# Score products of 48 by 128 instead of 48 by 64 in five pairs of a fused attention and feed-forward kernel

## The chip, the cores and the metric

The kernel runs on one core of a Trainium2 chip. The metric is the device time of one execution in microseconds (us), the median of repeated runs. Beside it stands one profiled execution, from which every duration below is taken.

## What is computed

The reference runs a gated linear attention over 4 batches, 8 heads, 768 positions and head size 48, and then a feed-forward block over the 3,072 tokens that come out:

```python
f = 1.0 / (1.0 + np.exp(-f_logit))
for t in range(S):
    state = f[:, :, t, :, None] * state + np.einsum('bhd,bhe->bhde', k[:, :, t], v[:, :, t])
    y[:, :, t] = np.einsum('bhd,bhde->bhe', q[:, :, t], state)
...
h = x @ w_in          # 3072 x 384 times 384 x 2048
g = h * np.cos(h)
return (g @ w_out).astype(np.float32)   # times 2048 x 384
```

The kernel doesn't step through the positions. It takes the sequence in pieces of 128, multiplies q and k by their running gate products, forms all products of q and k inside a piece (the scores), masks them, and carries a 48 by 48 state from piece to piece.

## The kernel before

**Tiling.** Two pieces of 128 positions make a pair; there are 12 pairs, three for each batch. Inside a pair each tile has 128 partitions of two neighbouring positions (e = 0 or 1), the 8 heads are halved into u = 0 and 1, and within a half the four heads are two head pairs (a = 0 or 1) of two heads (r = 0 or 1). The two pieces of a pair are g = 0 and 1. After the gates, `qk` holds q and k of one pair, each head widened from 48 to 64 columns by zeros.

**Turning q and k.** The scores need q and k with the head size on the partitions. For pairs 5 to 11 (`TURN_QK`) a transposing DMA on SP's queue does this (line 427). For pairs 0 to 4 TensorE does it: steps `tq` and `tk` are four products with the identity each (line 438), one for each e (in the code x) and a, into a bank of PSUM, and step `qkt` on DVE or ACT copies the result to the SBUF tile `qkt`. A head with r = 0 then lies on partitions 0 to 47, one with r = 1 on 64 to 111.

**Scores.** Step `sc` (line 460) computes for one pair and one half u the scores of four heads and two pieces. There are two such steps for each pair, so 24 in all, 10 of them for the five pairs that TensorE turns. Each is a loop over a, g, r and x: x is the position's parity on the side of k. The weights are 64 columns of k (48 rows), the moving data the 128 columns of q, and the result goes to partitions 64x to 64x + 63 of the PSUM bank that belongs to r. So one step is 16 matmuls with 16 weight loads, and four different quarters of TensorE's array are named in turn: rows by r, columns by x. Step `am` on DVE multiplies the scores by the mask.

**The other products of a pair.** Step `ps` (line 490) forms the products of k and v for the state from weights of 64 rows by 64 columns. Steps `y` and `yi` (line 543) form the output from weights of 128 rows by 32 columns; `yi` also reads q from `qkt`. The gates' running sums (lines 378 and 384) and the feed-forward products use the whole array.

**Feed-forward.** Steps `h` (line 610) and `o` (line 632) are the two large products, with a cosine on ACT (line 615) and the multiplication on DVE (line 582) between them.

**What sets the order.** The string `ORDER` lists every step with its engine and its PSUM bank or banks; `emit` writes them out in that order, and each engine works its own list in order. TensorE's steps of the attention are put between `h` and `o` steps. In the first 21 us there is not enough work, and steps `zf` multiply zeros (line 268) to keep TensorE running.

**Names that are used below:** `sc0.0`, `sc0.1`, `sc1.1`, `sc1.0`, `sc2.1`, `sc2.0`, `sc4.0`, `sc4.1`, `sc3.0`, `sc3.1` are the ten score steps of the turned pairs, in TensorE's order. In that order `ps0.1` stands right ahead of `sc0.1`, `ps2.1` right behind `sc2.1`, and `ps4.1` right ahead of `sc3.0`.

Of the kernel before, what the change touches and what calls it, by code (L numbers as in the profile page):

```python
# [10 lines left out]
BF16 = mybir.dt.bfloat16  # L11
# [4 lines left out]
B, H, S, D = 4, 8, 768, 48  # L16
# [173 lines left out]
def describe(nc, cpool, ppool, q, k, v, f_logit, moe_w_in, moe_w_out, out):  # L190
# [3 lines left out]
    def tl(shape, dt, name):  # L194
        return cpool.tile(shape, dt, name=name)

    def copy(e, o, i):
        (nc.scalar.copy if e == "ACT" else eng(e).tensor_copy)(out=o, in_=i)  # L198
# [6 lines left out]
    ident = tl([128, 128], BF16, "ident")  # L205
# [5 lines left out]
    if nc is not None:  # L211
# [5 lines left out]
        for r in range(2):  # L217
            s = slice(64 * r, 64 * r + 64)
# [96 lines left out]
    def pair(n):  # L315
# [50 lines left out]
        if not cut:  # L366
            G.step(f"ad{n}", ("POOL",), lambda e: eng(e).tensor_add(  # L367
                out=sp.ap[:, 0, :, 0:D], in0=soft.ap[:, :, 0, :], in1=soft.ap[:, :, 1, :]), reads=[soft], writes=[sp])
# [23 lines left out]
        for nm, dst, dh, sc, w in (("eb", bt, bth, -1.0, HB + 4), ("ei", bi, bih, 1.0, HB)):  # L392
            if cut:
                for u in us:
                    G.step(f"{nm}{n}.{u}", ("ACT",), lambda e, u=u, dh=dh, sc=sc, w=w: nc.scalar.activation(
                        out=dh[u].ap, in_=pcs[u].ap[:, 0:w], func=AF.Exp, scale=sc),
                        reads=[pcs[u]], writes=[dh[u]], table="E")
            else:
                G.step(f"{nm}{n}", ("ACT",), lambda e, dst=dst, sc=sc, w=w: nc.scalar.activation(
                    out=dst.ap, in_=pcs[0].ap[:, 0:2 * (HB + 4)].rearrange("p (u n) -> p u n", u=2)[:, :, 0:w],  # L400
# [5 lines left out]
        for u in us:  # L406
            for j, (nm, src, dec) in enumerate((("qm", qh[u], bth[u]), ("km", kh[u], bih[u]))):
                G.step(f"{nm}{n}.{u}", ("POOL", "DVE"), lambda e, u=u, j=j, src=src, dec=dec: eng(e).tensor_mul(  # L408
                    out=qkp[u][j].ap[:, :, :, 0:D], in0=swap(src.ap),
# [11 lines left out]

        qkt = [Val(qktS), Val(qktS)]
        turned = n in TURN_QK
        qkv = lambda u: qkt[u].ap.rearrange("p (j e a g n) -> p j a g e n", j=2, a=2, g=2, e=2)
        for u in us:
            if turned:
                G.step(f"tq{n}.{u}", ("SP",), lambda e, u=u: nc.sync.dma_start_transpose(
                    out=qkt[u].ap.rearrange("p (b n) -> p b n", n=C),
                    in_=qk.ap[:, u].rearrange("p j e h d -> p (j e h d)")),
                    reads=[qkp[u][0], qkp[u][1]], writes=[qkt[u]])  # L430
                continue
            pt = Val(p1)

            def tr(e, u, j, pt):
                o = pt.ap.bitcast(BF16).rearrange("p (j e a n) -> p j e a n", j=2, e=2, a=2)
                for x in range(2):
                    for a in range(2):
                        nc.tensor.transpose(out=o[:, j, x, a, :], identity=ident,  # L438
                                            in_=qkp[u][j].ap[:, x, 2 * a:2 * a + 2, :].rearrange("p h d -> p (h d)"))
            for j in range(2):  # L440
                G.step(f"t{'qk'[j]}{n}.{u}", ("PE",), lambda e, u=u, j=j, pt=pt: tr(e, u, j, pt),
                       reads=[qkp[u][j]], writes=[pt], sums=True)
            G.step(f"qkt{n}.{u}", ("DVE", "ACT"), lambda e, u=u, pt=pt: copy(e, qkt[u].ap, pt.ap.bitcast(BF16)),
                   reads=[pt], writes=[qkt[u]])
# [5 lines left out]
        for u in us:  # L450
            sc = Val(p2)

            def scores(e, u=u, sc=sc):
                o = sc.ap.rearrange("p (r b n) -> p r b n", r=2, n=C)
                for a in range(2):
                    for g in range(2):
                        for r in range(2):
                            for x in range(2):
                                s, t = slice(64 * r, 64 * r + D), slice(64 * x, 64 * x + 64)
                                nc.tensor.matmul(o[t, r, 2 * a + g, :].rearrange("p (e n) -> p e n", e=2),  # L460
                                                 lhsT=qkv(u)[s, 1, a, g, x, :], rhs=qkv(u)[s, 0, a, g, :, :],
                                                 start=(a == 0 and g == 0), stop=(a == 1 and g == 1))
            G.step(f"sc{n}.{u}", ("PE",), scores, reads=[qkt[u]], writes=[sc])
            if n in CHUNKS:
                for g in range(2):
                    G.step(f"am{n}.{u}{g}", ("DVE",), lambda e, u=u, g=g, sc=sc: nc.vector.tensor_mul(
                        out=am[u].ap.rearrange("p r (a g) n -> p (r a) g n", g=2)[:, :, g, :],
                        in0=sc.ap.rearrange("p (y g m) -> p y g m", g=2, m=C)[:, :, g, :],
                        in1=pmask.rearrange("p a n -> p (a n)")[:, None, :].broadcast_to([128, 4, C])),
                        reads=[sc], writes=[amp[u][g]])  # L470
                continue
            G.step(f"am{n}.{u}", ("DVE",), lambda e, u=u, sc=sc: nc.vector.tensor_mul(  # L472
                out=am[u].ap.rearrange("p r b n -> p (r b) n"), in0=sc.ap.rearrange("p (y m) -> p y m", m=C),
                in1=pmask.rearrange("p a n -> p (a n)")[:, None, :].broadcast_to([128, 8, C])),
                reads=[sc], writes=[am[u]])
# [22 lines left out]
        for g in gs:  # L498
            view = lambda g=g: ps[g].ap[:, 0:HB].rearrange("p (a n) -> p a n", n=D)
            dense, new, sums = Val(sdS), Val(szS), ps[g].part(None)  # L500
            if carried is not None:
                G.step(f"st{n}.{g}", ("DVE",), lambda e, view=view, S0=carried: nc.vector.tensor_add(
                    out=view(), in0=view(), in1=S0.ap), reads=[sums, carried], writes=[sums])
# [68 lines left out]
        x = Val(xS)  # L572
# [73 lines left out]
    for n in range(PAIRS):  # L646
        pair(n)
# [108 lines left out]
```

## Time and profile before

| | us |
|---|---|
| median of 3 runs | 181.26 (181.18 to 181.77) |
| the profiled execution's own time | 180.39 |
| its span, first to last instruction | 178.1 |
| so outside the span | 2.3 |
| granted TensorE clock | 1.00 of full speed in all 40 slices |

In the profile, PE is the matmul side of TensorE and PEld its weight loads, which overlap the matmuls. Matmuls are pipelined, so the time of one (some 0.22 us for 128 moving columns) is a latency; how fast they follow one another is read from the timeline, where a row merges a run of like instructions: start, time from the first start to the last end, line, shape and count. "issue" names idle time of an engine that waited for nothing that the profile shows. DMA queue 1 carries the kernel's own transfers; the packets of the kind "instruction" are listed apart.

### The profile page before, as it was taken

The page shows a single profiled execution, that of the slowest core. Times are in us where ns is not written, and L with a number is a line of the kernel's source. Part 1 is how long each engine was busy: PE and PEld are TensorE (multiplying, and loading weights), DVE is VectorE, ACT ScalarE, POOL GpSimd, SP SyncE. Part 2 cuts the span into 40 slices and gives each one's busy share as a digit, 9 for nine tenths or more (in the row PEclk, how much of TensorE's full clock was granted, in tenths as well). Part 3 has the DMA queues.
Part 4 walks back from the last instruction along what each step waited for, and adds up shares of the span by engine and source line. Part 5 has one row for each costly group of instructions (what it writes and reads, how often), then busy time and mean ns, then how long its engine had stood idle before and what let it go on. Part 6 is the DMA issues. An engine that isn't in the chain of part 4 may idle for free.

```text
span 178.1 us, 5999 instructions
## 1 busy us (share of the span) xinstructions
PE 169.9 (95%) x2546; PEld 124.9 (70%) x2550; DVE 135.5 (76%) x196; ACT 137.7 (77%) x205; POOL 100.4 (56%) x128
## 2 busy tenths in 40 slices
PE   7999999999999989999999999899999999999991
PEld 2555598766877678866688766787867778687770
DVE  5588829988799988899799789889998746547211
ACT  5789998899999999999999897798962646364221
POOL 4044979975797969985979979899401000000000
PEclk9999999999999999999999999999999999999999
DMA  5999999999999969999999979883730030010044
GB/s 139 260 270 303 376 349 347 315 296 263 261 255 264 261 139 219 284 196 256 253 245 306 171 184 275 148 203 59 147 77 4 0 123 13 4 44 0 0 172 140
DMA packets 72282, 33.94 MB, mean 191 GB/s; under 512 B 65344, under 2 KB 70720, under 8 KB 72256
## 3 DMA queue, kind: packets, MB, share of 16 engines
q1 hardware_dynamic: 72256, 33.56, 76.9%
q8 instruction: 20, 0.33, 0.8%
q14 instruction: 6, 0.05, 0.1%
HBM read 25.17 MB, written 4.72 MB: 168 GB/s over the span
## 4 chain that ended last, share of the span: by engine, by line
PE 83%; ACT 5%; DVE 5%; DMA 3%; issue 2%; ACTq 0%; DVEq 0%
PE ps L610 34%; PE ps L632 33%; PE ps L543 5%; PE ps L460 3%; DVE am L472 3%; PE ps L438 2%; PE ps L490 2%; PE ps L268 2%; DMA f<-in_f_logit_dram 1%; PE ps L378 1%; DMA out_dram<-ot 1%; ACT sp L337 1%; ACT f L333 1%; ACT vt L198 1%; DVE g L582 1%
## 5 line engine op out<-in xcount | busy, mean ns | idle before, releaser
L582 DVE TENSOR_TENSOR g<-ps,co 128x1024 bf16<-128x1024 f32 x48 | 60.2, 1310 | 18.7 <-ACT co L615 18.5
L632 PE MATMUL ps<-w_out_bf,g 128*128 128x384 bf16 (+1 forms) x400 | 69.2, 320 | 0.0
L610 PE MATMUL ps<-x,w_in_bf 128*128 128x256 bf16 (+1 forms) x624 | 66.6, 264 | 0.5 <-DVE g L582 0.4
L615 ACT ACTIVATE co<-ps,halfpi 128x1024 bf16<-128x1024 f32 x48 | 51.7, 1113 | 18.4 <-PE ps L610 16.3
L610 PEld LDWEIGHTS <-w_in_bf 128*128 128x128 bf16 x624 | 56.5, 98 | 8.3 <-issue 0.5
L632 PEld LDWEIGHTS <-g 128*128 128x128 bf16 x400 | 37.0, 98 | 20.0
L472 DVE TENSOR_TENSOR am<-ps,pmask 128x1024 bf16<-128x1024 f32 x22 | 26.0, 1216 | 1.5 <-PE ps L460 1.4
L408 POOL TENSOR_TENSOR qk<-q,b 128x384 bf16<-128x384 f32 x18 | 17.8, 1007 | 3.2 <-DVE q L342 2.3
L408 POOL TENSOR_TENSOR qk<-k,bi 128x384 bf16<-128x384 f32 x16 | 16.3, 1029 | 5.3 <-issue 2.0
L198 POOL COPY vt<-vb 64x384 bf16<-64x384 bf16 x31 | 15.8, 520 | 2.0 <-PE ps L543 0.6
L268 PE MATMUL ps<-zero 128*128 128x512 bf16 x40 | 12.7, 430 | 1.5 <-DVE zero L204 1.2
L198 ACT COPY ot<-ps 128x384 f32<-128x384 f32 (+1 forms) x13 | 5.8, 451 | 8.8 <-PE ps L632 7.1
L517 POOL TENSOR_TENSOR sz<-sd,half 128x384 bf16<-128x384 bf16 x10 | 8.2, 828 | 7.6 <-DVE sd L507 7.2
L198 POOL CAST vb<-v 128x768 bf16<-128x768 f32 x9 | 7.4, 825 | 8.9 <-DMA v<-in_v_dram 8.8
L333 ACT ACTIVATE f<-f 128x768 f32<-128x768 f32 (+1 forms) x14 | 10.3, 748 | 2.7 <-DMA f<-in_f_logit_dram 2.6
L198 DVE CAST x<-ps 128x384 bf16<-128x384 f32 x16 | 8.5, 552 | 4.8 <-PE ps L543 4.7
L367 POOL TENSOR_TENSOR sp<-ls 128x384 bf16<-128x384 f32 x10 | 10.0, 1000 | 2.3 <-ACT ls L337 2.1
L198 DVE COPY ot<-ps 128x384 f32<-128x384 f32 (+1 forms) x13 | 6.7, 521 | 4.6 <-PE ps L632 4.5
L345 POOL TENSOR_TENSOR q<-f,q 128x384 f32<-128x384 f32 x9 | 9.4, 1039 | 0.6 <-ACT f L348 0.2
L460 PE MATMUL ps<-qkt 48*64 48x128 bf16 x384 | 9.0, 220 | 0.3 <-DVE qkt L198 0.3
L198 ACT COPY vt<-vb 64x384 bf16<-64x384 bf16 x17 | 8.5, 508 | 0.3
L507 DVE TENSOR_TENSOR sd<-ps,b 128x192 bf16<-128x192 f32 x20 | 7.1, 354 | 2.1 <-PE ps L490 1.3
(66 smaller groups left out, 189.4 us busy)
## 6 DMA issues: line engine op xcount, KB each, us to landing
v<-in_v_dram SPq DMA_DIRECT2D x12, 384.0 KB, 5.9
out_dram<-ot SPq DMA_DIRECT2D x22, 192.0 KB, 3.0
f<-in_f_logit_dram SPq DMA_DIRECT2D x10, 384.0 KB, 5.8
q<-in_q_dram SPq DMA_DIRECT2D x10, 384.0 KB, 5.6
k<-in_k_dram SPq DMA_DIRECT2D x10, 384.0 KB, 6.3
g<-in_moe_w_in_dram SPq DMA_DIRECT2D x4, 768.0 KB, 8.4
g<-in_moe_w_out_dram SPq DMA_DIRECT2D x4, 768.0 KB, 9.3
f<-in_f_logit_dram SPq DMA_DIRECT2D x4, 192.0 KB, 3.7
```

Of the source, the lines that this page charges most:

```text
L198: (nc.scalar.copy if e == "ACT" else eng(e).tensor_copy)(out=o, in_=i)
L268: G.step(f"zf{i}", ("PE",), lambda e, dump=dump: nc.tensor.matmul(dump.ap, lhsT=zero[:, 0:128], rhs=zero, start=True, stop=True), writes=[ ...
L333: nc.scalar.activation(out=flat(t.ap), in_=flat(t.ap), func=AF.Exp, scale=-1.0)
L345: eng(e).tensor_mul(out=w.ap[:, :, 0, :], in0=t.ap[:, :, 1, :], in1=w.ap[:, :, 0, :])
L367: G.step(f"ad{n}", ("POOL",), lambda e: eng(e).tensor_add(out=sp.ap[:, 0, :, 0:D], in0=soft.ap[:, :, 0, :], in1=soft.ap[:, :, 1, :]), read ...
L408: G.step(f"{nm}{n}.{u}", ("POOL", "DVE"), lambda e, u=u, j=j, src=src, dec=dec: eng(e).tensor_mul(out=qkp[u][j].ap[:, :, :, 0:D], in0=swap ...
L460: nc.tensor.matmul(o[t, r, 2 * a + g, :].rearrange("p (e n) -> p e n", e=2), lhsT=qkv(u)[s, 1, a, g, x, :], rhs=qkv(u)[s, 0, a, g, :, :], ...
L472: G.step(f"am{n}.{u}", ("DVE",), lambda e, u=u, sc=sc: nc.vector.tensor_mul(out=am[u].ap.rearrange("p r b n -> p (r b) n"), in0=sc.ap.rear ...
L582: nc.vector.tensor_mul(out=o.rearrange("p b (n e) -> p b e n", e=2), in0=ph.ap.rearrange("p (b e n) -> p b e n", e=2, n=64), in1=co.ap.rea ...
L610: nc.tensor.matmul(ph.ap[:, i * T:(i + 1) * T].rearrange("p (g t) -> p g t", t=C), lhsT=w_in_bf[:, kk, f0:f0 + 128], rhs=xa[:, :, kk, :], ...
L615: G.step(f"co{m}.{j}", ("ACT",), lambda e, ph=ph, co=co: nc.scalar.activation(out=co.ap, in_=ph.ap, func=AF.Sin, bias=halfpi), reads=[ph], ...
L632: nc.tensor.matmul(po.ap[:, 0:c1 - c0], lhsT=gap[:, j, i * C:(i + 1) * C], rhs=w_out_bf[:, j, c0:c1], start=(po.first and j == 4 * s), sto ...
```

## The change

In the five pairs that TensorE turns, `qkt` is laid out with the two parities of one head pair and piece side by side (j, a, g, e, n in place of j, e, a, g, n). The turning product now writes its 128 columns as two pieces of 64. With that, the 128 columns of k for one head and piece are contiguous, and the score step loads them as one set of weights: eight products of 48 by 128 in place of sixteen of 48 by 64, each writing all 128 partitions. For pairs 5 to 11 the layout and the sixteen products stay. `ORDER` isn't touched.

```diff
         qkt = [Val(qktS), Val(qktS)]
         turned = n in TURN_QK
-        qkv = lambda u: qkt[u].ap.rearrange("p (j e a g n) -> p j a g e n", j=2, a=2, g=2, e=2)
+        lay = "p (j e a g n) -> p j a g e n" if turned else "p (j a g e n) -> p j a g e n"
+        qkv = lambda u: qkt[u].ap.rearrange(lay, j=2, a=2, g=2, e=2)
...
             def tr(e, u, j, pt):
-                o = pt.ap.bitcast(BF16).rearrange("p (j e a n) -> p j e a n", j=2, e=2, a=2)
+                o = pt.ap.bitcast(BF16).rearrange("p (j a g e n) -> p j a g e n", j=2, a=2, g=2, e=2)
                 for x in range(2):
                     for a in range(2):
-                        nc.tensor.transpose(out=o[:, j, x, a, :], identity=ident,
+                        nc.tensor.transpose(out=o[:, j, a, :, x, :], identity=ident,
                                             in_=qkp[u][j].ap[:, x, 2 * a:2 * a + 2, :].rearrange("p h d -> p (h d)"))
...
                         for r in range(2):
-                            for x in range(2):
-                                s, t = slice(64 * r, 64 * r + D), slice(64 * x, 64 * x + 64)
-                                nc.tensor.matmul(o[t, r, 2 * a + g, :].rearrange("p (e n) -> p e n", e=2),
-                                                 lhsT=qkv(u)[s, 1, a, g, x, :], rhs=qkv(u)[s, 0, a, g, :, :],
+                            s = slice(64 * r, 64 * r + D)
+                            for t, w in [(slice(64 * x, 64 * x + 64), qkv(u)[s, 1, a, g, x, :]) for x in range(2)] if turned else [
+                                    (slice(0, 128), qkv(u)[s, 1, a, g, :, :].rearrange("p e n -> p (e n)"))]:
+                                nc.tensor.matmul(o[t, r, 2 * a + g, :].rearrange("p (e n) -> p e n", e=2), lhsT=w,
+                                                 rhs=qkv(u)[s, 0, a, g, :, :],
                                                  start=(a == 0 and g == 0), stop=(a == 1 and g == 1))
```

No engine's steps change places, but TensorE's list becomes shorter: 16 rows less for each of the ten steps, so 4,942 rows in place of 5,102. (In the changed kernel all lines behind the diff stand two further down: 460 becomes 462, 490 becomes 492, 543 becomes 545, 610 becomes 612.)

First place, TensorE where `sc2.1` ends and `ps2.1` begins. Before:

```order
L460 LDWEIGHTS qkt_0_130
L460 MATMUL ps_1_166<-qkt_0_130 64x128
L490 LDWEIGHTS qk_0_121
L490 MATMUL ps_2_167<-vb_0_124,qk_0_121 64x48
L490 LDWEIGHTS qk_0_121
```

Now, at the same place:

```order
L462 LDWEIGHTS qkt_0_130
L462 MATMUL ps_1_166<-qkt_0_130 128x128
L492 LDWEIGHTS qk_0_121
L492 MATMUL ps_2_167<-vb_0_124,qk_0_121 64x48
L492 LDWEIGHTS qk_0_121
```

The neighbours are the same; the score product beside the 64 by 64 product now spans all columns of the array.

Second place, TensorE's list counted from its start, rows 1,978 to 1,982, which lie behind the ten steps. Before, inside step `y3`:

```order
L543 MATMUL ps_3_168<-am_2_137,vt_0_127 32x128
L543 LDWEIGHTS vt_0_127
L543 MATMUL ps_3_168<-am_2_137,vt_0_127 32x128
L543 LDWEIGHTS vt_0_127
L543 MATMUL ps_3_168<-am_2_137,vt_0_127 32x128
```

Now, in the same rows, feed-forward products:

```order
L612 MATMUL ps_3_168<-x_1_147,w_in_bf_163 128x256
L612 LDWEIGHTS w_in_bf_163
L612 MATMUL ps_2_167<-x_0_146,w_in_bf_163 128x256
L612 LDWEIGHTS w_in_bf_163
L612 MATMUL ps_2_167<-x_0_146,w_in_bf_163 128x256
```

Behind the ten steps every instruction of TensorE stands 160 rows earlier than before.

## The prediction

> **What bounds the kernel now.** I read the page first: busy shares, then the chain that ended last.
>
> ```profile
> span 178.1 us, 5999 instructions
> ...
> PE 169.9 (95%) x2546; PEld 124.9 (70%) x2550; DVE 135.5 (76%) x196; ACT 137.7 (77%) x205; POOL 100.4 (56%) x128
> ...
> PE 83%; ACT 5%; DVE 5%; DMA 3%; issue 2%; ACTq 0%; DVEq 0%
> ```
>
> TensorE is busy for 95% of the span and holds 83% of the chain. Time taken from TensorE's list should come off the end, time added should go on it. "issue" is 2% of the chain, time in which nothing visible was waited for. Next the waits of TensorE alone (sum, times, longest):
>
> ```profile
> PE ps L543 <- issue: 1.3, 2, 0.8
> PE ps L268 <- DVE zero L204: 1.2, 1, 1.2
> PE ps L610 <- DVE g L582: 0.4, 1, 0.4
> PE ps L268 <- issue: 0.3, 2, 0.2
> PE ps L460 <- DVE qkt L198: 0.3, 1, 0.3
> ```
>
> The second row lies at the start and the last three before 28 us. What TensorE loses in its dense part is the first row: two stalls inside `y` and `yi` (L543), with no producer named.
>
> **The score steps themselves.** The timeline of TensorE (start, time, line, shape, count) shows how fast matmuls follow one another:
>
> ```profile
> 10.86 0.42 PE L460 MATMUL ps<-qkt 48*64 48x128 bf16 x16
> ...
> 16.97 0.62 PE L438 MATMUL ps<-ident,qk 128*128 128x128 bf16 x8
> ...
> 38.12 0.42 PE L460 MATMUL ps<-qkt 48*64 48x128 bf16 x16
> 38.37 0.41 PE L490 MATMUL ps<-vb,qk 64*64 64x48 bf16 x16
> ...
> 40.12 0.42 PE L460 MATMUL ps<-qkt 48*64 48x128 bf16 x16
> 40.47 0.34 PE L632 MATMUL ps<-w_out_bf,g 128*128 128x384 bf16 x1
> ...
> 59.32 0.44 PE L490 MATMUL ps<-vb,qk 64*64 64x48 bf16 x32
> 59.60 0.74 PE L460 MATMUL ps<-qkt 48*64 48x128 bf16 x32
> ```
>
> And the groups by line, with the mean of one matmul and one load:
>
> ```profile
> L460 PE MATMUL ps<-qkt 48*64 48x128 bf16 x384 | 9.0, 220 | 0.3 <-DVE qkt L198 0.3
> L438 PE MATMUL ps<-ident,qk 128*128 128x128 bf16 x80 | 7.2, 219 | 0.2 <-DVE qk L408 0.2
> ...
> L460 PEld LDWEIGHTS <-qkt 48*64 48x64 bf16 x384 | 6.2, 106 | 3.0 <-issue 1.6 <-DVE qkt L198 1.2
> L438 PEld LDWEIGHTS <-qk 128*128 128x128 bf16 x80 | 5.6, 98 | 2.7 <-DVE qk L408 0.8 <-POOL qk L408 0.3 <-issue 0.2
> ```
>
> Eight whole-array matmuls of 128 columns take 0.62; less one latency of 0.22, seven spacings are 0.40, so 0.057 each. Sixteen score matmuls take 0.42, so fifteen spacings are 0.20, or 0.013 each: four quarters of the array run together, four rounds of some 0.055. The new step has eight matmuls whose weights fill half the rows and all columns, r = 0 and r = 1 in turn into different banks. Run two at a time, that is again four rounds of 0.055. **Removed:** 80 loads and 80 matmuls; **gained in the array:** nothing. The bounds of this term: the two halves together, 0; the halves one after the other, 8 x 0.057 = 0.46 in place of 0.23 (4 x 0.057), so +0.23 for a step. I take 0, since r = 0 and r = 1 are among the four that run together now.
>
> A load of 128 columns has 98 ns against 106 for 64, and loads run beside matmuls; first loads may save up to 0.01 a step, bounds 0 to -0.1 over ten, I take 0. [...]
>
> **Writing the turned tile in two pieces** (80 matmuls): no row shows a split write. The nearest is L460, which reads its moving data in two pieces and has 220 ns against 219. Bounds: 0 to 80 x 1 ns = 0.1; I take 0. The copy `qkt` and `am` read and write as many elements as before.
>
> **Changed neighbours.** From L460 to L490 at 38.12 the next start comes 0.25 later; from L460 to the whole-array L632 at 40.12 it is 0.35. So a change in how the array is divided costs 0.10, and L460 and L490 now share a division. After the change they don't, at three places: 11.83, 38.37 and 59.60. The first lies among the zero products (L268), which are filler and hide it; if they didn't, 0.1 more. Cost +0.2, bounds 0 to 0.3.
>
> **The two stalls move with the list.** The timeline around them, and a piece of the chain for the pace of L543:
>
> ```profile
> 63.14 0.23 PE L543 MATMUL ps<-am,vt 128*32 128x128 bf16 x4
> 63.84 0.57 PE L543 MATMUL ps<-am,vt 128*32 128x128 bf16 x28 [0.48 <-issue]
> ...
> 110.85 0.29 PE L543 MATMUL ps<-qkt,sz 128*32 128x128 bf16 x8
> 111.95 0.41 PE L543 MATMUL ps<-qkt,sz 128*32 128x128 bf16 x16 [0.81 <-issue]
> ...
> 143.06 1.68 PE ps L543 x112
> ```
>
> At 1.68 / 112 = 0.015 each, the matmul at 63.84 was due at 63.14 + 4 x 0.015 = 63.20: lost 0.64. The one at 111.95 was due at 110.97: lost 0.98. Together **1.62 us**. What they wait for is in the DMA views: the page's row of the queue that carries instructions, then the same row in the windows 61.10 to 61.25 and 109.25 to 109.35:
>
> ```profile
> q8 instruction: 20, 0.33, 0.8%
> ...
> q8 instruction: 1, 0.02, 47.0%
> ...
> q8 instruction: 1, 0.02, 77.1%
> ```
>
> TensorE's 2,546 + 2,550 instructions over 20 packets are 255 a packet, so I take a packet for 256 instructions of TensorE's list. Each stall ends 2.6 to 2.7 after such a packet started. The windows say whether both stand at the same place in a packet (time, then busy and count of PE and PEld; a window also counts what is in flight at its start, which at 63.84 and 111.95 is nothing):
>
> ```profile
> 63.84:111.95 48.11, 47.30 (x767) 35.83 (x767) 41.91 (x56) 44.55 (x65) 40.98 (x50) 1.00 1.05 229
> ...
> 59.51:63.84 4.33, 3.85 (x154) 2.88 (x143) 4.19 (x8) 4.29 (x11) 3.95 (x6) 1.00 1.11 254
> 107.92:111.95 4.03, 3.22 (x136) 2.35 (x137) 3.65 (x6) 2.92 (x7) 3.97 (x6) 1.00 1.22 275
> 83.76:88.57 4.81, 4.81 (x126) 3.06 (x127) 4.00 (x5) 4.76 (x12) 4.67 (x7) 1.00 1.19 261
> 130.24:135.39 5.15, 5.15 (x133) 3.51 (x136) 4.61 (x8) 2.15 (x6) 0.83 (x1) 1.00 0.26 51
> ...
> 110.24:116.17 5.93, 5.12 (x144) 4.30 (x133) 5.08 (x10) 3.85 (x7) 5.27 (x7) 1.00 0.91 186
> 86.82:92.08 5.26, 5.26 (x129) 4.06 (x128) 4.28 (x9) 5.15 (x10) 5.05 (x7) 1.00 1.01 236
> ```
>
> From stall to stall there are 767 + 767 = 1,534 instructions, and six packets are 1,536. So both are the first instruction of a packet. Counting 128 loads back, the packet ahead of each began at 59.51 and 107.92 (second and third row): 4.33 and 4.03 from one packet's first instruction to the next one's, while the work between took only 3.7 and 3.05. My reading: when TensorE enters a packet, the next is ordered, and it is there 4.0 to 4.3 later; a packet full of tiny matmuls is used up sooner. The next shortest, 4.81 and 5.15 (rows four and five), ran without a stall.
>
> Now the list is 160 shorter from 60 us on, and the packets' edges fall 160 instructions further on in the old order. Counting the old trace that way, the edge ahead of 63.84 falls to 62.47, and the next to 70.25, among L610 products: nearly 8 us. The edges around the second stall fall to 110.24 and 116.17 (row six): 5.93 less the lost 0.98 is 4.95. Of the others behind 30 us the shortest is 5.26 (row seven). All are over 4.33, the tightest by 0.6, so both stalls go: **-1.62**. Does the gain last? Behind 64 us the largest waits are:
>
> ```profile
> DVE g L582 <- ACT co L615: 15.5, 14, 3.3
> ACT co L615 <- PE ps L610: 15.1, 17, 3.5
> ```
>
> DVE waits for ACT, and ACT for TensorE, so both come earlier with TensorE. Next to be late would be `g` before the `o` steps; bounds: all of 1.62 lasts, or 1.0.
>
> **Sum** against the profiled execution: 180.39 + 0 + 0.2 - 1.6 = 179.0. The median stands 0.87 above that execution; with the same -1.4 it becomes **179.9**.
>
> **The rivals.**
> - *The stalls stay or come back elsewhere.* The packet's lead is seen at only two stalls. If it needs 5 to 6 us at times, 110.24 or 86.82 stalls by up to 1, and the gain is spent: 181.3, from 180.8 to 181.6. For it: TensorE's loads have more small "issue" waits that I don't explain. If one stall goes alone: 181.26 + 0.2 - 0.64 or - 0.98, about 180.6.
> - *The halves take turns.* Each of the ten steps costs 0.23 more; the six from 38 us on lie on TensorE's dense path, so +1.4 to +2.3. The sum is then 181.3 to 182.2 with -1.4 for the rest, and 182.8 with all ten steps and only 1.0 gained from the stalls (-0.8 + 2.3). It ends slower once the steps cost 0.54 more than the rest gains: 1.9 together, or 0.19 of the 0.23 each. For it: no row shows half the rows with all columns. Against it: the four quarters at 0.013. [...]
> - *Fewer starts are cheaper.* If a start and not the array set the pace of 0.013, eight would spread over 0.10 in place of 0.20: 0.1 a step, 1.0 over ten, 178.9. Against it: L490 at 59.32 has 32 matmuls of 0.19 in 0.44, so 0.008 between starts. [...]
>
> **How the numbers follow.** Both stalls gone: 0.52, 179.4 to 180.4. One gone: 0.16, about 180.6. Stay or come back: 0.16. Turns: 0.14, a fifth of it under 181.8. Fewer starts: 0.02. A measurement tells 0.3%, 0.54 us, from no change: faster means under 180.72. Faster: 0.52 + 0.11 of the second case + 0.02 = 0.65; same: 0.05 + 0.14 + 0.03 = 0.22; slower: the rest, 0.13, nearly all of it turns. The range, 179.2 to 181.9, leaves out most of the turns, the case of fewer starts, and a margin of the first.
>
> **What would show it.** Right: no "issue" row of 0.4 or more on L545 in TensorE's waits; 19 instruction packets in place of 20; a step of eight still 0.40 to 0.42; the start after `sc2.1` 0.35 later. Wrong: a step of eight over 0.5 (turns), or an "issue" wait on another line (the packet's lead is longer than 4.3).

## The result, and the profile after

The changed kernel takes 178.71 us (median of 4 runs, 178.65 to 179.66) against 181.49 (181.18 to 181.77) before: ratio 0.986, 95% interval 0.982 to 0.990. The ratios here and below leave out runs that are more than 1.5% above the fastest of their kernel, while medians and ranges have all runs. It was forecast faster by 1.4 us; it is faster by 2.8, and 178.71 lies below the range.

The page of the changed kernel, the lines that answer to those of before:

```profile
span 177.4 us, 5843 instructions
...
PE 170.8 (96%) x2470; PEld 124.8 (70%) x2470; DVE 136.0 (77%) x196; ACT 137.7 (78%) x205; POOL 100.1 (56%) x128
...
q8 instruction: 19, 0.31, 0.8%
```

80 matmuls and 80 loads are gone (four matmuls have no record in the profile of before, so it counts 2,546 where it counts 2,550 loads), TensorE's busy time isn't smaller (170.8 us against 169.9), and the queue of instructions has 19 packets in place of 20. The waits of TensorE (sum, times, longest):

```profile
PE ps L268 <- DVE zero L204: 1.2, 1, 1.2
PE ps L634 <- ACT w_out_bf L198: 0.8, 1, 0.8
PE ps L612 <- POOL w_in_bf L198: 0.4, 1, 0.4
PE ps L378 <- ACT sp L337: 0.3, 2, 0.2
```

No "issue" row is left (rows of under 0.15 us aren't listed). Where the two stalls were, TensorE's timeline (start, time, line, shape, count) now runs through:

```profile
63.77 0.63 PE L545 MATMUL ps<-am,vt 128*32 128x128 bf16 x32
64.23 0.68 PE L545 MATMUL ps<-qkt,sz 128*32 128x128 bf16 x36
64.73 0.62 PE L545 MATMUL ps<-am,vt 128*32 128x128 bf16 x32
...
111.00 0.52 PE L545 MATMUL ps<-qkt,sz 128*32 128x128 bf16 x24
111.34 0.62 PE L545 MATMUL ps<-am,vt 128*32 128x128 bf16 x32
111.79 0.51 PE L545 MATMUL ps<-qkt,sz 128*32 128x128 bf16 x24
112.13 0.62 PE L545 MATMUL ps<-am,vt 128*32 128x128 bf16 x32
```

This profiled execution has a wait of its own, the second row of the waits above: `o` products wait 0.8 us near 38.7 us for the cast of `w_out`, and ACT's cast waited 2.0 us for a transfer. It is the slowest of the four runs (179.66; the others have 178.65 to 178.76). So the two profiled spans, 178.1 and 177.4, show only 0.7 us of the 2.8: the profile of before is from a run 1.1 us below its kernel's median (180.39 against 181.49), and that of after from one 0.95 above.

### The profile page after: what moved, and what is told of

Read it like the earlier page. It is cut to its first block, busy times and chain, and to the rows that moved or that the text cites. A ratio compares the mean times of both kernels' runs of the same rounds, so it can differ in the third digit from the quotient of the medians.

```text
span 177.4 us, 5843 instructions
## 1 busy us (share of the span) xinstructions
PE 170.8 (96%) x2470; PEld 124.8 (70%) x2470; DVE 136.0 (77%) x196; ACT 137.7 (78%) x205; POOL 100.1 (56%) x128
## 4 chain that ended last, share of the span: by engine, by line
PE 75%; DMA 11%; ACT 3%; DVE 3%; SPq 2%; POOL 2%; issue 1%; DVEq 0%; POOLq 0%
PE ps L634 33%; PE ps L612 28%; DMA g<-in_moe_w_in_dram 5%; DMA v<-in_v_dram 5%; PE ps L545 4%; PE ps L462 3%; SPq L286 2%; PE ps L492 2%; PE ps L268 2%; POOL w_in_bf L198 2%; DMA f<-in_f_logit_dram 2%; PE ps L439 1%; DVE am L474 1%; PE ps L378 1%; DVE qk L408 1%
## 5 line engine op out<-in xcount | busy, mean ns | idle before, releaser
L198 POOL COPY vt<-vb 64x384 bf16<-64x384 bf16 x31 | 15.3, 503 | 1.4
L268 PE MATMUL ps<-zero 128*128 128x512 bf16 x44 | 13.9, 426 | 1.2 <-DVE zero L204 1.2
L355 POOL TENSOR_TENSOR k<-k,f 128x384 f32<-128x384 f32 (+1 forms) x7 | 6.8, 973 | 4.1 <-DMA k<-in_k_dram 2.0
L462 PE MATMUL ps<-qkt 48*64 48x128 bf16 (+1 forms) x304 | 8.9, 219 | 0.1
```

The lines of the kernel that those rows point to most:

```text
L268: G.step(f"zf{i}", ("PE",), lambda e, dump=dump: nc.tensor.matmul(dump.ap, lhsT=zero[:, 0:128], rhs=zero, start=True, stop=True), writes=[ ...
```

## The experiments

Two theories. **P**: the time lies in where TensorE's list is cut into packets of 256 instructions (an estimate: 1,534 instructions from stall to stall, over six packets); the change matters because it makes the list shorter. **S**: the eight wider products are cheaper themselves.

### e1: the kernel before, once more

> The unchanged kernel once more, for a second profile. Both theories expect 181.5 us. Theory P (the time lies where TensorE's list is cut into packets of 256 instructions): the same two issue waits at L543 near 63.8 and 112 us, at the same instructions, and 20 packets; what its usual run has above the first profile (181.5 against 180.4) should show as a longer or a third wait. Theory S (the eight wider products are cheaper themselves) says nothing of these waits.

Measured: 181.64 (10 runs, 180.5 to 183.2), ratio to before 1.004 (0.9995 to 1.009). Waits and timeline of TensorE in this second profile:

```profile
PE ps L543 <- issue: 1.8, 2, 1.3
...
63.36 0.23 PE L543 MATMUL ps<-am,vt 128*32 128x128 bf16 x4
64.92 0.57 PE L543 MATMUL ps<-am,vt 128*32 128x128 bf16 x28 [1.33 <-issue]
```

Same two places: 4 matmuls of this block, then the stall, then 28, as in the first profile. But the first stall is 1.33 in place of 0.48, the second 0.47 in place of 0.81. The places are fixed, the lengths are not. The two stalls together are 0.5 longer than in the first profile, most of the 0.77 that this run is longer (181.16 against 180.39).

### e2: sixteen products, cuts of the changed kernel

`EXTRA = 48` pairs of load and product: the first 16 fillers are cut into four.

```diff
-            G.step(f"zf{i}", ("PE",), lambda e, dump=dump: nc.tensor.matmul(
-                dump.ap, lhsT=zero[:, 0:128], rhs=zero, start=True, stop=True), writes=[dump])
+            more = min(3, max(0, EXTRA - 3 * i))
+            edge = [0, 128, 256, 384, 512] if more == 3 else [0, 192, 384, 512] if more == 2 else [0, 256, 512] if more == 1 else [0, 512]
+
+            def fill(e, dump=dump, edge=edge):
+                for c0, c1 in zip(edge, edge[1:]):
+                    nc.tensor.matmul(dump.ap[:, c0:c1], lhsT=zero[:, 0:128], rhs=zero[:, c0:c1], start=True, stop=True)
+            G.step(f"zf{i}", ("PE",), fill, writes=[dump])
```

> The kernel before with its sixteen products, and 96 instructions more at the start (16 of the filler products of 512 zero columns cut into four of 128), so that behind 20 us the packets are cut at the same products as in the changed kernel. Theory P: faster by 1.6 to 2.8 us although more is issued, 178.7 to 179.9, no issue wait over 0.3 at L548. Theory S: no gain, 181.5 to 181.7, the waits somewhere else or gone without effect.

Measured: 179.91 (10 runs, 179.47 to 180.79) against 181.24 of before on that chip, ratio 0.994 (0.990 to 0.997). Faster with 96 instructions more and the old products, but by less than the change, and by less than the 1.6 that P asked for at least. Its waits and timeline show where time was lost again:

```profile
PE ps L638 <- ACT w_out_bf L199: 0.7, 1, 0.7
PE ps L616 <- issue: 0.4, 1, 0.4
...
22.57 0.62 PE L616 MATMUL ps<-x,w_in_bf 128*128 128x128 bf16 x8 [0.42 <-issue]
```

Nothing stands at L549 (the old L543). A new stall of 0.42 stands at 22.57, where a cut now falls, and the first feed-forward product starts at 21.87 in place of 21.43, since the cut fillers hold back the first turning product (8.76 in place of 8.16). The first row is a wait for the cast of `w_out`, as in the first profile of the changed kernel.

### e3: the changed kernel, once more

> The changed kernel once more, for a second profile. Both theories expect 178.7 us. If the wait of 0.8 us for the cast of w_out near 38.7 us in the first profile (179.66 us) is a chance of that run, it is gone here and the span is near 176.4.

Measured: 178.43 (4 runs, 178.32 to 179.01), ratio 0.987 (0.980 to 0.993). The wait for the cast of `w_out` is gone, so it was a chance of that run. The span is 176.8 and not 176.4: this profiled run is again the slowest of its four, with another small wait of the packets:

```profile
110.53 0.30 PE L545 MATMUL ps<-qkt,sz 128*32 128x128 bf16 x8 [0.31 <-issue]
```

The score steps stand clear here:

```profile
38.08 0.40 PE L462 MATMUL ps<-qkt 48*128 48x128 bf16 x8
38.41 0.43 PE L492 MATMUL ps<-vb,qk 64*64 64x48 bf16 x16
...
40.18 0.40 PE L462 MATMUL ps<-qkt 48*128 48x128 bf16 x8
40.51 0.66 PE L634 MATMUL ps<-w_out_bf,g 128*128 128x384 bf16 x3
...
60.12 0.62 PE L462 MATMUL ps<-qkt 48*128 48x128 bf16 x16
60.67 0.34 PE L378 MATMUL ps<-sp,incl 128*128 128x384 bf16 x1
```

Eight products take 0.40, sixteen took 0.42. Less one latency of 0.22, the eight have 0.18 for seven spacings, 0.026 each, where whole-array products had 0.057: the halves run together. To `ps2.1` it is now 0.33 in place of 0.25, to the whole-array product 0.33 in place of 0.35.

### e4: eight products, cuts of the kernel before

The edit of e2 on the changed kernel, with `EXTRA = 80`.

> The changed kernel with 160 instructions more in the filler at the start (80 pairs of load and product), so that behind 60 us the packets are cut at the same products as in the kernel before. Theory P: the two stalls in y and yi are back near 64 and 112 us, and the time is 1.6 to 2.8 us above the changed kernel, 180.3 to 181.5. Theory S: within 0.2 of the changed kernel, 178.7 to 178.9.

Measured: 182.43 (10 runs, 180.24 to 186.5), ratio to before 1.003 (0.998 to 1.008). The median is above the 180.3 to 181.5 that P expected. The gain is gone although the products are the wide ones. The stalls are back, after 4 and after 8 matmuls of the same blocks:

```profile
65.08 0.57 PE L551 MATMUL ps<-am,vt 128*32 128x128 bf16 x28 [0.29 <-issue]
...
112.89 0.41 PE L551 MATMUL ps<-qkt,sz 128*32 128x128 bf16 x16 [0.51 <-issue]
```

The profile also has 1.0 us of waiting for a weight cast near 22.5 us, which is not a packet's; so the size of the loss here is not the stalls' alone.

### e5: sixteen products, harmless cuts, fillers that cost nothing

`EXTRA = 5`: each of the first eight fillers is cut into six.

```diff
-            G.step(f"zf{i}", ("PE",), lambda e, dump=dump: nc.tensor.matmul(
-                dump.ap, lhsT=zero[:, 0:128], rhs=zero, start=True, stop=True), writes=[dump])
+            cuts = 1 + EXTRA if i < 8 else 1
+            edge = [512 * c // cuts for c in range(cuts + 1)]
...
```

> The kernel before with its sixteen products, and 80 instructions more, all in the first eight filler products (512 zero columns cut into six pieces), where TensorE waits for its first input anyway. Counted along the old trace, no packet behind 25 us is then used up in less than 4.9 us. Theory P: the two stalls go, 178.6 to 179.4 us, nearly all that the change brought, and the times lie closer together than before (179.5 to 182.6). Theory S: 181.2 to 181.7.

Measured: 179.04 (6 runs, 178.81 to 179.44) against 181.43 (17 runs, 179.3 to 182.95), ratio 0.987 (0.982 to 0.991). That is the change's own ratio, with the old products and 80 instructions more in place of 160 fewer. The runs also lie closer together, within 0.6 us in place of 3.7. The three shortest packets behind 25 us, as windows (time, then busy and count of PE and PEld):

```profile
58.20:63.47 5.27, 5.27 (x129) 3.52 (x130) 5.13 (x8) 5.21 (x14) 4.64 (x7) 1.00 1.02 244
88.28:93.18 4.90, 4.90 (x131) 4.26 (x131) 3.81 (x10) 4.47 (x8) 4.25 (x6) 1.00 1.26 269
104.92:110.58 5.66, 5.66 (x147) 3.61 (x137) 5.04 (x6) 5.24 (x11) 5.54 (x9) 1.00 1.05 250
```

TensorE is busy through all of each: no packet came late. What it still pays is one early stall:

```profile
22.87 0.28 PE L616 MATMUL ps<-x,w_in_bf 128*128 128x128 bf16 x2 [0.75 <-issue]
```

### e6: the layout alone

```diff
-                            for t, w in [(slice(64 * x, 64 * x + 64), qkv(u)[s, 1, a, g, x, :]) for x in range(2)] if turned else [
-                                    (slice(0, 128), qkv(u)[s, 1, a, g, :, :].rearrange("p e n -> p (e n)"))]:
+                            for t, w in [(slice(64 * x, 64 * x + 64), qkv(u)[s, 1, a, g, x, :]) for x in range(2)]:
```

> The new layout of q and k and the split write of the turned tile, but sixteen products of 48 by 64 in every pair, so the list is as long as before. Theory P: as before, 181.2 to 181.7, with both issue waits at L545. If the layout itself were worth something (contiguous columns of q), faster by up to 0.5.

Measured: 181.79 (10 runs, 180.08 to 183.97), ratio 1.001 (0.996 to 1.006): as before. The profiled run is one of the long ones (183.76). Its waits:

```profile
PE ps L544 <- issue: 2.9, 2, 1.5
...
PE ps L611 <- issue: 1.1, 1, 1.1
```

Both old stalls are there, 2.9 together in place of the 1.3 of the first profile, and one of 1.1 early, at 24.50.

### e7: eight products, the worst cut

The edit of e5 on the changed kernel, with `EXTRA = 7`.

> The changed kernel with 112 instructions more in the first eight filler products (cut into eight pieces each), chosen for the worst cut. Counted along the trace, three packets are then used up in 3.1, 3.3 and 3.7 us. Theory P: three stalls, near 64, 89 and 111 us, where the second is at a place at which no kernel stalled so far; 181 to 182.5 us, slower than before is possible although the score products are the wide ones. Theory S: 178.4 to 178.8.

Measured: 185.48 (4 runs, 182.41 to 186.28), ratio to before 1.012 (1.002 to 1.021): slower than before with the wide products, and above the 181 to 182.5 that P expected. The ratio rests on two of the four runs.

```profile
66.00 0.24 PE L551 MATMUL ps<-am,vt 128*32 128x128 bf16 x4 [1.08 <-issue]
...
116.20 0.52 PE L551 MATMUL ps<-am,vt 128*32 128x128 bf16 x24 [2.59 <-issue]
```

The stall at the place that no kernel had stalled at so far was there, but small: 0.09 us near 91. The one near 116 was far longer than I had expected, and behind it TensorE was slow for a while, as the windows show (the granted clock is the third number from the end):

```profile
113.00:117.00 4.00, 1.41 (x74) 1.11 (x63) 1.85 (x6) 0.90 (x2) 1.61 (x3) 1.00 1.08 155
117.00:121.00 4.00, 4.00 (x24) 2.70 (x21) 2.98 (x5) 2.93 (x5) 3.94 (x6) 0.57 0.36 112
121.00:125.00 4.00, 4.00 (x38) 3.43 (x36) 2.46 (x2) 3.54 (x5) 3.92 (x5) 1.00 0.69 154
```

Behind the stall the clock is 0.57 for four microseconds, and 24 matmuls are done where 38 are done in the next four. Of the pages of before, after and e5 to e8 only this one has slices under 0.9 ahead of the span's end (0.7 and 0.8, from 115 to 124 us), so it isn't shown that the stall caused it.

### e8: eight products, the longest shortest packet

The edit of e5 on the changed kernel, with `EXTRA = 14`.

> The changed kernel with 224 instructions more in the first eight filler products (cut into fifteen pieces each), so that the shortest packet behind 25 us lasts 5.6 us where the changed kernel's shortest has 4.9. Theory P: the last chance stalls go, 178.2 to 178.7. If the many small pieces make TensorE late for its first input, 0.2 to 0.5 more.

Measured: 178.44 (4 runs, 178.02 to 179.73), ratio 0.985 (0.979 to 0.992). Beside e3's ratio of 0.987 that is no difference that these runs can tell. TensorE's waits in its profile (span 175.8) name no "issue" at all. No experiment beat the changed kernel.

### All stalls together

From the trace's records of instruction packets, and counting loads and matmuls to find where each packet is entered: every stall of the dense part, in us.

| run | packet entered at | the next one's transfer starts after | from that start to its first instruction | idle |
|---|---|---|---|---|
| before | 59.51 | 1.66 | 2.67 | 0.48 |
| before | 107.92 | 1.38 | 2.65 | 0.81 |
| e1 | 59.73 | 2.62 | 2.57 | 1.33 |
| e1 | 109.00 | 0.98 | 2.71 | 0.47 |
| e3 | 104.34 | 3.58 | 2.61 | 0.31 |
| e4 | 60.83 | 1.70 | 2.55 | 0.29 |
| e4 | 109.16 | 1.17 | 2.56 | 0.51 |
| e6 | 60.90 | 2.77 | 2.62 | 1.53 |
| e6 | 110.36 | 1.76 | 2.78 | 1.32 |
| e7 | 60.95 | 2.42 | 2.64 | 1.08 |
| e7 | 87.45 | 1.09 | 2.55 | 0.09 |
| e7 | 110.32 | 3.30 | 2.58 | 2.59 |

At 256 to a packet, all twelve lie on the first instruction of one. The last part is nearly constant, 2.55 to 2.78. What varies is how long it takes until the transfer starts: 0.98 to 3.58. The three early stalls (22.57 in e2, 22.87 in e5, 24.50 in e6) ended 2.3 to 2.4 after a packet's transfer had started.

The packets show at one more place, the end of the kernel. The chain's last pieces before, and then in the first profile of the changed kernel:

```profile
167.04 4.24 PE ps L632 x28
171.31 0.49 ACT ot L198
171.81 2.13 DMA out_dram<-ot
174.04 0.54 ACT ot L198 x2
...
167.10 7.19 PE ps L634 x56
174.31 0.32 ACT ot L198
```

Before, the last copies wait for a store. In that profile an instruction packet starts at 170.47, 3.5 us ahead of the last matmul's start, and the two stores then under way land 3.0 and 3.1 us after their issue. In the profiles without a packet there they take 1.9 to 2.0. Over all ten profiles: where the last packet starts 1.8 to 3.5 ahead of the last matmul (before, e1, e4, e6, e7), it is 4.1 to 4.5 us from that matmul's start to the end of the span; where it starts 9.4 to 10.6 ahead (after, e2, e3, e5, e8), it is 3.4. So the change also gains 0.7 at the end. In the ten profiles that goes with where the last packet falls; no run moved this one packet alone.

## Why the prediction was right or wrong

**The mechanism: right, but not whole.** The forecast said that TensorE stalls where a packet full of tiny matmuls is used up before the next is there, that the change moves the cuts, and that both stalls go. e5 shows it from one side (old products, other cuts: the full gain, 0.987 against 0.986), e4 and e7 from the other (new products, bad cuts: no gain, 1.003, or slower than before, 1.012). Theory S falls with e5 and e4. What the forecast left out is the end, where a packet among the last stores went with 0.7 more.

**The score products, term 0: right.** A step of eight takes 0.40 against 0.42. "The halves take turns" asked for over 0.5 and falls. "Fewer starts are cheaper" expected the starts to spread over 0.10; 0.40 less one latency of 0.22 is 0.18. It falls too.

**The split write, term 0: nothing speaks against it.** e6 has it, and the ratio is 1.001, but its interval of 0.5% either way can't tell 0.1 us. The turning matmuls themselves have a mean of 219 ns in e3, as before.

**The changed neighbours, +0.2: too dear.** At `sc2.1` the 0.10 came as 0.08 in e3. At 59.60 `sc3.0` also starts 0.10 later behind `ps4.1` (0.38 in place of 0.28, in e8), but the two steps there then take 0.56 in place of 0.67, so nothing of it is left. Setting each feed-forward matmul of e8 against the same one of the first profile, the difference moves by +0.10 at 38.7 and by 0.03 in all from there to 61.7. So the term was 0.1.

**The packets, -1.62: the step that failed, by its size.** In the execution in which I had measured the two stalls, 0.64 and 0.98 lost, the term is right: against it, e8's feed-forward matmuls come 0.66 earlier behind the first place and 1.00 behind the second, 1.66 together, and it lasts to the last matmul. Two things were missing in the sum.

- I wrote that the median stands 0.87 above that execution "with the same -1.4". That offset was no constant beside the stalls. The profile was of a run with short stalls; the second profile has 1.33 and 0.47 of idle time, e6's 1.53 and 1.32. By the same comparison the stalls cost 0.86 more in e1 at the first place and 0.34 less at the second, so 2.2 in a run of 181.16, near the median.
- The end was put at nothing, and it gave 0.7 more (4.12 from the last matmul to the end of the span before, 3.42 after).

e5, which takes the stalls and the late packet at the end away and keeps the products, gives the two as 181.43 - 179.04 = 2.4, or 1.7 to 3.2 by its interval, and pays 0.75 early in its profile on top. With 2.4 or more in place of 1.62 the forecast would have been 179.1 or less. The spread was in sight: the runs of before lay up to 1.4 above the profiled one, and the range's lower end came from the first profile's stalls alone.

**What was right only in part.** "All are over 4.33, the tightest by 0.6, so both stalls go": they went, but the lead isn't bounded by 4.33. Over the twelve stalls it took 3.6 to 6.2 from entering a packet to the next one's first instruction. e3 has a stall in a packet that had lasted 5.65, after a transfer that started 3.58 late. The rival that a stall comes back elsewhere thus happens in some executions, at 0.3 us. 19 packets were forecast and 19 came. The count of 255 a packet was helped by luck: six packets back from the first stall, the transfer that started at 13.30 begins with about the 440th instruction, so the twenty don't hold just the list. The 1,534 from stall to stall is what carries the 256.

**Still open.** Why a transfer starts after 1 us in one execution and 3.6 in another wasn't tried. "When TensorE enters a packet, the next is ordered" can't be the whole rule: counted the same way, a packet of the first profile starts at 152.35, 2.4 ahead of the first instruction of the one before it. The twelve stalls' packets were entered between 59 and 111 us. In the first profile's two the DMA share is 1.11 and 1.22, while the packet entered at 130.24, with a share of 0.26, lasted only 5.15 and ran through. So the kernel's own transfers may hold the packets back; no run tried it. Also open is how much of the medians' 2.8 lies in the first 50 us, where waits for weights differ from run to run (0.8 in the first profile of after, none in the second).

## What to carry to other kernels

An instruction can cost more than its time on the engine: here TensorE's list came in packets, and where a run of tiny matmuls had used up one packet before the next was there, TensorE stood idle for 0.09 to 2.59 us (the twelve stalls of the table). Where "issue" waits stand in a dense run of small matmuls, count the instructions from one to the next; if they are a multiple of the packet (an estimated 256 here), some tens of instructions more or fewer far ahead, even useless ones in idle time, can move the cut. Here 80 did, and were worth as much as the whole change (e5, 0.987 against 0.986). See also whether a packet falls among the last stores (in the five profiles where one did, the end was 0.7 to 1.1 us longer). And when a stall's length hangs on a transfer, take it from several executions (0.48 and 1.33 us at the same place here), and suspect it first in whatever separates the profiled run from the median.

## What the runs showed of the hardware

- From the first stall of before to the second TensorE had 1,534 instructions, and six instruction packets were moved; 256 to a packet is an estimate from these two numbers. From the start of a packet's transfer (1.13 and 1.23 us long at the two stalls of before) to its first instruction it took 2.55 to 2.78 us in all twelve stalls of the table; in these twelve the transfer itself started 0.98 to 3.58 us after TensorE entered the packet before.
- An instruction packet's transfer that started among the last stores went with stores of 2.9 to 3.1 us in place of 1.9 to 2.0 (before, e7), and with 4.1 to 4.5 us from the last matmul to the end in place of 3.4 (five profiles against five).
- After a stall of 2.6 us the granted TensorE clock was 0.57 in the window from 0.8 to 4.8 us behind its end (e7, one profile). After the 1.3 and 1.5 us stalls of e6 it was 1.00 in the windows from 66 to 70 and from 115 to 119.
- Eight matmuls on half the rows and all columns, 48 by 128, with the two halves of the rows in turn, took 0.40 us (e3), where eight on the whole array took 0.62 (before): 0.026 from start to start against 0.057, so two ran in the time of one.
